# Second layer of a fused attention and mixture-of-experts kernel: 15 of 18 token tiles in Strassen's seven products, gated values through DRAM

## The chip, the cores and the metric

The kernel runs on one core of a Trainium2 chip. The metric is the device time of one execution in microseconds. Engines are named as in the profile: TensorE (PE; PEld for its weight loads), VectorE (DVE), ScalarE (ACT), GpSimd (POOL), and SyncE (SP), which only issues DMAs.

## The reference, cut to what matters

Attention (4 batches, 8 heads, 576 positions, 64 per head, causal, with a bias from a cumulative sum) gives x of 2304 tokens by 512. A mixture of 8 experts follows, two experts a token (512 to 1024 to 512). Its output goes into a second, dense layer, which is where the change lies:

```python
def _moe2_ref(x, w_gate, w_val, w_out):      # x [2304, 512], w_gate, w_val [512, 1536], w_out [1536, 512]
    gate = 1.0 / (1.0 + np.exp(-(x @ w_gate)))
    val = x @ w_val
    return (gate * val @ w_out).astype(np.float32)
```

## The kernel before, in words

Every matrix product is done in three passes of a reduced float32 format: an operand is split into a high part (a ScalarE copy) and a low part (a subtraction, on VectorE or GpSimd), and TensorE adds high x high, high x low and low x high in PSUM. So each product costs three matmuls and each operand one copy and one subtraction.

Four stages follow one another: attention with the gating of the experts (to about 279 us), the experts (`moe`, to 722 us), a branch for overfull experts that is normally not taken (`overflow`, L438 on), and the second layer (`moe2`, from 725.7 us to the end). Tokens go to their experts and back by indirect DMAs through DRAM; `ys` has two rows for each token, one per expert, to be added.

The experts run in units of one 128-wide block of one expert's hidden width: `mm1` (L214, matmuls at L225 to L227) for 640 slots, then `mm2` of the unit before (L239 to L241). The last expert is split: its first three slot tiles in one pass of eight units, its other two in the next eight, so that the second layer's first three token tiles can be read and transposed (`after`, L334) while the last units run. In the order of the code each unit also loads a later unit's weights (`load`: DMA on SP, high part on ScalarE at L151, low part mostly on GpSimd at L152), and runs a few steps of `background`, a generator that converts the second layer's weights, which arrive as 64-bit floats, in 24 halves of blocks (`convert`, L274): seven steps on VectorE to a float32, then the high part on ScalarE (L306) and the low part on VectorE (L309). Of the 12 blocks (128 of the hidden width each: 512 columns of w_gate, 512 of w_val, 512 of w_out) the first `RES` = 5 stay in SBUF (`wa`); 7 are stored to `w2d` in DRAM in split form and read back into `wc` by GpSimd's queue when the second layer begins (L577).

`moe2` works in 72 units: six groups of three token tiles (384 tokens), 12 blocks each. A unit n does `mm1` (2 x 4 x 3 matmuls of 384 columns into two PSUM banks, L539 to L541; sigmoid on ScalarE, the product and the split into `gh` and `gl` on VectorE and ScalarE) and then `mm2` of unit n-1 (3 tiles x 3 matmuls of 512 columns, L557 to L559), which adds into three PSUM banks over the 12 blocks. The next group's tiles are read (`fetch_sum`: a load on SP, then an adding load on GpSimd's queue) in units 1 to 3 and transposed by TensorE and split (`feed`) in units 7 to 9. All instructions of an engine run in the order in which the code issues them, and so do the DMAs of one queue; a buffer is taken again when its last user is done.

Of the kernel before, what the change touches and what calls it, by code (L numbers as in the profile page):

```python
# [19 lines left out]
FF2 = 1536  # L20
# [33 lines left out]
RES, AFTER = 5, 4  # L54
# [9 lines left out]
def attn_moe_moe2_kernel(ctx: ExitStack, tc: tile.TileContext, q, k, v, s, wgn, noise, wcat, w2cat, out):  # L64
# [66 lines left out]
    w2d = tc.dram_tile([FB2 - RES, 128, 2, FF2], F32, name="w2d")  # L131
# [7 lines left out]
    with res:  # L139
        w2, x0, first = moe(tc, moe_pools, res, gates, stage, ring, w1, late, count, xs, ys, wcat, w2cat, w2d, identf, identr)  # L140
        overflow(tc, xs, ys, wcat, carry, over, identf)
        moe2(tc, w2, x0, first, ys, w2d, identr, out)
# [13 lines left out]
def moe(tc, pools, res, gates, stage, ring, W, late, count, xs, ys, wcat, w2cat, w2d, identf, identr):  # L156

# [3 lines left out]
    wa = []  # L161
    with pools as ctx:
# [17 lines left out]
        def start(n):  # L180
            e, f = jobs[n][0:2]
            lo = nc.vector if n in LOW_DVE else nc.gpsimd
            pool, name = (w0, f"w{f}") if n < FB and f >= 4 else (ring, "w")
            LD[n] = weights(nc, tw[0] if n >= n_all - 2 else stage, pool, wcat, e, f, name, lo)
            next(LD[n])
# [88 lines left out]
        def convert(f, g, half=FF2 // 2):  # L274
# [8 lines left out]
            v = cv.tile([128, half], F32, name="cv")  # L283
# [15 lines left out]
            if f < RES:  # L299
                hi, lo = (wa[f][:, i, g * half:(g + 1) * half] for i in range(2))  # L300
            else:
                w = cv.tile([128, 2, half], F32R, name="cw", bufs=2)
                hi, lo = w[:, 0], w[:, 1]
            yield
            yield
            nc.scalar.activation(hi, v, AF.Copy)  # L306
            yield
            yield
# [3 lines left out]
            if f >= RES:  # L312
                stores.append(lambda: nc.sync.dma_start(w2d[f - RES][:, :, g * half:(g + 1) * half], f32(w)))
            yield
# [19 lines left out]
        def after(j):  # L334

            if j == 0:
                first.extend(x0.tile([128, 4, CT * 128], F32R, name=m) for m in ("xh", "xl"))
                for i in range(CT):
                    y[i] = fetch(nc, x0, ys, i, reads)
            for i in range(CT):  # L340
                if j == AFTER + i:
                    p = ps.tile([128, 512], F32, name=f"y{i}")
                    nc.vector.tensor_tensor(y[i][:, 0], y[i][:, 0], y[i][:, 1], op=OP.add)
                    turns[i] = feed(nc, y[i][:, 0], p, identf, *(x[:, :, i * 128:(i + 1) * 128] for x in first))
                if AFTER + i < j < AFTER + i + 3:
                    next(turns[i])

# [26 lines left out]
        for n in range(FB, n_all):  # L374
            e, f = jobs[n][0:2]
            if n == 2 * FB + 1:
                held.close()
                ra = res.enter_context(tc.tile_pool(name="res_a", bufs=1, side="right", reuse_waits="tile"))
                wa += [ra.tile([128, 2, FF2], F32R, name=f"wa{f2}") for f2 in range(RES)]
# [14 lines left out]
            if n == tail - 2:  # L394
                tw.append(ctx.enter_context(tc.tile_pool(name="tw", bufs=2, side="right", reuse_waits="tile")))
                for i in range(tail + 4, n_all):
                    start(i)
# [11 lines left out]
            if n == tail - 8:  # L409
# [3 lines left out]
                x0 = res.enter_context(tc.tile_pool(name="x0", bufs=1, side="right", reuse_waits="tile"))  # L413
        mm2s(n_all - 1)
        for j in range(FB, AFTER + CT + 3):
            after(j)
    rc = res.enter_context(tc.tile_pool(name="res_c", bufs=1, side="right", reuse_waits="tile"))
    for f2 in range(RES, FB2):
        wa.append(rc.tile([128, 2, FF2], F32R, name=f"wc{f2}"))
    return wa, x0, first  # L420
# [67 lines left out]
def fetch(nc, pool, ys, t, reads):  # L488

    y = pool.tile([128, 2, DM], F32, name="y", bufs=3)  # L490
# [612 lines left out]
```

## Time and profile before

| | |
|---|---|
| median of 3 runs | 1187.55 us (1185.42 to 1188.81) |
| the profiled execution: time, span | 1189.59 us, 1187.6 us |
| TensorE busy | 1136.2 us (96%) |
| VectorE, ScalarE, GpSimd busy | 592.5 us (50%), 433.8 us (37%), 291.1 us (25%) |
| mean granted TensorE clock | 0.984 |
| DMA | 162.59 MB, mean 137 GB/s |
| second layer | 725.7 us to the end |

Matmuls overlap, so a single one's duration (394 ns for 512 columns) is longer than the distance from one to the next, and TensorE's rate is read from the distances. A line's idle time is the time that its engine waited just before it. The granted clock is a share of 2.4 GHz: 1.00 is that level and 0.5 is 1.2 GHz.

### The profile page before, as it was taken

How to read it: one execution, taken by the hardware profiler on the slowest of the kernel's cores; microseconds unless marked ns; L12 is line 12 of the kernel's file. 1: busy time of each engine (PE TensorE's matmuls, PEld its weight loads, DVE VectorE, ACT ScalarE, POOL GpSimd, SP SyncE). 2: the span in 40 equal slices, each digit the busy share in tenths (PEclk: the TensorE clock that was granted, in tenths of full speed). 3: DMA queues.
4: the chain of work that ended last, by engine and by line, in shares of the span. 5: the costliest groups of instructions: out<-in, count | busy, mean ns of one | idle time of the engine just before them, and what ended most of it. 6: DMA issues, size and time to landing. Idle time of an engine off the chain costs nothing.

```text
span 1187.6 us, 17005 instructions
## 1 busy us (share of the span) xinstructions
PE 1136.2 (96%) x6625; PEld 998.2 (84%) x6625; DVE 592.5 (50%) x1030; ACT 433.8 (37%) x910; POOL 291.1 (25%) x286
## 2 busy tenths in 40 slices
PE   7998888799999999999999998999999999999998
PEld 4766655588999889888888997999999999999997
DVE  6787768473478988889882223121221221212111
ACT  6877666433334343333343432122121211212111
POOL 2103242423335353535353643000000000000000
PEclk8999989899999999999999999999999999999999
DMA  6898464426435546576744343803011030020000
GB/s 228 277 334 266 163 210 129 144 71 220 163 127 183 179 165 243 175 261 225 272 179 153 118 165 148 296 1 81 1 57 23 1 80 1 29 52 1 27 1 27
DMA packets 52606, 162.59 MB, mean 137 GB/s; under 512 B 6594, under 2 KB 7106, under 8 KB 51620
## 3 DMA queue, kind: packets, MB, share of 16 engines
q1 hardware_dynamic: 43060, 127.35, 32.3%
q0 software_dynamic: 9312, 33.90, 8.6%
q8 instruction: 54, 0.88, 0.3%
q14 instruction: 36, 0.29, 0.1%
q10 hardware_dynamic: 144, 0.16, 0.0%
HBM read 111.06 MB, written 46.44 MB: 133 GB/s over the span
## 4 chain that ended last, share of the span: by engine, by line
PE 68%; DVE 11%; DMA 7%; issue 5%; POOL 4%; ACT 3%; SPq 1%; another core or an unknown queue 0%; POOLq 0%; ACTq 0%; DVEq 0%
PE h L539 8%; PE h L541 8%; PE h L540 8%; PE o L558 4%; PE o L557 4%; PE o L559 4%; PE h L225 3%; PE h L227 3%; PE h L226 3%; PE y L239 3%; PE y L240 3%; PE y L241 3%; PE av L813 3%; PE tp L784 3%; DMA ys<-yo,row 3%
## 5 line engine op out<-in xcount | busy, mean ns | idle before, releaser
L152 POOL TENSOR_TENSOR w<-wraw,w 128x1024 fp32r<-128x1024 f32 x62 | 153.5, 2482 | 238.3 <-ACT w L151 233.3
L544 DVE TENSOR_TENSOR sg<-h,sg 128x384 f32<-128x384 f32 x72 | 40.2, 558 | 303.7 <-PE h L541 293.4
L225 PE MATMUL h<-xh,w 128*128 128x320 f32 (+2 forms) x512 | 162.1, 317 | 4.1 <-DVE hl L229 4.1
L227 PE MATMUL h<-xh,w 128*128 128x320 f32 (+2 forms) x512 | 158.6, 310 | 0.0
L226 PE MATMUL h<-xl,w 128*128 128x320 f32 (+2 forms) x512 | 158.3, 309 | 0.0
L239 PE MATMUL y<-w,hh 128*128 128x512 f32 x320 | 126.5, 395 | 0.0
L240 PE MATMUL y<-w,hh 128*128 128x512 f32 x320 | 126.3, 395 | 0.0
L241 PE MATMUL y<-w,hl 128*128 128x512 f32 x320 | 126.1, 394 | 0.0
L539 PE MATMUL h<-xh,wc 128*128 128x384 f32 x336 | 114.0, 339 | 0.0
L541 PE MATMUL h<-xh,wc 128*128 128x384 f32 x336 | 113.0, 336 | 0.0
L540 PE MATMUL h<-xl,wc 128*128 128x384 f32 x336 | 112.9, 336 | 0.0
L151 ACT ACTIVATE w<-wraw 128x1024 fp32r<-128x1024 f32 x68 | 72.0, 1059 | 104.1 <-PE y L241 79.9
L225 PEld LDWEIGHTS h<-xh,w 128*128 128x128 f32 x512 | 96.5, 188 | 8.1 <-DVE hl L229 6.4
L543 ACT ACTIVATE sg<-h 128x384 f32<-128x384 f32 x72 | 35.5, 493 | 184.8 <-PE h L541 184.8
L229 DVE SCALAR_TENSOR_TENSOR hl<-h,hh 128x320 fp32r<-128x320 f32 (+2 forms) x128 | 59.0, 485 | 86.4 <-ACT hh L228 86.4
L226 PEld LDWEIGHTS h<-xl,w 128*128 128x128 f32 x512 | 96.6, 189 | 1.6
L227 PEld LDWEIGHTS h<-xh,w 128*128 128x128 f32 x512 | 96.4, 188 | 0.0
L228 ACT ACTIVATE hh<-h 128x320 fp32r<-128x320 f32 (+2 forms) x128 | 54.9, 435 | 111.3 <-PE h L227 107.1
L546 ACT ACTIVATE gh<-sg 128x384 fp32r<-128x384 f32 x72 | 37.7, 524 | 155.9 <-DVE sg L544 155.9
L500 POOL DMA_DIRECT2D y<-ys x15 | 13.4, 995 | 294.7 <-PE h L541 284.9
L539 PE MATMUL h<-xh,wa 128*128 128x384 f32 x240 | 80.9, 337 | 3.3 <-ACTq L442 3.3
L541 PE MATMUL h<-xh,wa 128*128 128x384 f32 x240 | 80.8, 337 | 0.0
(202 smaller groups left out, 2420.0 us busy)
## 6 DMA issues: line engine op xcount, KB each, us to landing
wraw<-in_wcat_dram SPq DMA_DIRECT2D x68, 512.0 KB
dw<-in_w2cat_dram SPq DMA_DIRECT2D x24, 768.0 KB
w2d<-cw SPq DMA_DIRECT2D x14, 768.0 KB
wc<-w2d POOLq DMA_DIRECT2D x7, 1536.0 KB
xs<-zt SPq DMA_DIRECT2D x40, 258.0 KB
xr<-xs SPq DMA_DIRECT2D x40, 258.0 KB
qr<-in_q_dram SPq DMA_DIRECT2D x15, 640.0 KB
kr<-in_k_dram SPq DMA_DIRECT2D x15, 576.0 KB
```

Of the source, the lines that this page charges most:

```text
L151: nc.scalar.activation(w[:, 0], r, AF.Copy)
L152: (lo or nc.gpsimd).tensor_tensor(w[:, 1], r, f32(w[:, 0]), op=OP.subtract)
L225: nc.tensor.matmul(p, w[:, 0, k], xh[:, c, c0], start=c == 0, stop=False)
L226: nc.tensor.matmul(p, w[:, 0, k], xl[:, c, c0], start=False, stop=False)
L227: nc.tensor.matmul(p, w[:, 1, k], xh[:, c, c0], start=False, stop=c == 3)
L229: nc.vector.scalar_tensor_tensor(hl[:, c0], p, 0.0, f32(hh[:, c0]), op0=OP.max, op1=OP.subtract)
L239: nc.tensor.matmul(y, hh[:, k], w[:, 0, 512:], start=n % FB == 0, stop=False)
L240: nc.tensor.matmul(y, hh[:, k], w[:, 1, 512:], start=False, stop=False)
L241: nc.tensor.matmul(y, hl[:, k], w[:, 0, 512:], start=False, stop=n % FB == FB - 1)
L539: nc.tensor.matmul(q, w[:, 0, s], xh[:, c], start=c == 0, stop=False)
L540: nc.tensor.matmul(q, w[:, 0, s], xl[:, c], start=False, stop=False)
L541: nc.tensor.matmul(q, w[:, 1, s], xh[:, c], start=False, stop=c == 3)
```

## The change

The second layer's first three token tiles (the first group) are computed as before. The other 15 tiles get their first product in seven block products for eight: the sum over 512 is halved (gate rows g1, g2 and value rows v1, v2, each 256 by 128 for a block), and each token tile is halved into 64 and 64 tokens. The weights' operands are g1, g2, v2 and four sums s1 to s4; the tokens' operands are four halves and three differences. They are kept for two groups of tiles, of eight and of seven (`sizes`), so a product's matmuls have 512 or 448 columns.

A turn of the new loop does one block for one of the two groups, 24 turns in all. It issues the read of the next turn's weights (`combos`: 512 KB from `w2f` on SP; four GpSimd sums of 256 columns; high parts on ScalarE, 1792 columns in three pieces; low parts on VectorE), does six of its products on four PSUM banks, and the last product of the turn before (`pend`) as its third. Partial sums leave PSUM by three ScalarE copies (p1, p5, u2) and three VectorE additions; two sigmoids and two multiplications give the gated values, which SP stores to `gs` in DRAM. During the first eight-tile group's turns the second group's tiles are read, transposed and combined (`combine`). With turn 12 the first group's operands are given up and all of w_out is read into their place (`wo`). After the turns, `final` does each tile's output product alone (36 matmuls of 512 columns), with its gated values read from `gs` (`get`) and split (`parts`) two tiles ahead.

The converted weights are no longer split and kept in `moe`: every half block goes unsplit to `w2f`, and the first group reads and splits blocks as it goes (`block`), the first three in the last eight units of the experts. There the second layer's tiles are read by two loads each (`both`), and of the four last weights one more shares the raw buffers.

```diff
-            if f < RES:
-                hi, lo = (wa[f][:, i, g * half:(g + 1) * half] for i in range(2))
...
-            nc.scalar.activation(hi, v, AF.Copy)
...
-            nc.vector.tensor_tensor(lo, v, f32(hi), op=OP.subtract)
...
+            stores.append(lambda: nc.sync.dma_start(w2f[f][:, g * half:(g + 1) * half], v))
...
-                for i in range(tail + 4, n_all):
-                    start(i)
+                for i in (4, 5, 7):
+                    start(tail + i)
+            if n == tail + 2:
+                start(tail + 6)
...
+    def combos(self, u):
+        nc, r = self.nc, self.stage.tile([128, 1024], F32, name="wraw")
+        nc.sync.dma_start(r, self.w2f[u % FB2][:, 0:1024])
+        yield
+        g1, g2, v1, v2 = (r[:, i * 256:(i + 1) * 256] for i in range(4))
+        s = self.raw()
+        s1, s2, s3, s4 = (s[:, i * 256:(i + 1) * 256] for i in range(4))
+        for o, x, y, op in ((s1, v1, v2, OP.add), (s2, s1, g1, OP.subtract), (s3, g1, v1, OP.subtract),
+                            (s4, g2, s2, OP.subtract)):
+            nc.gpsimd.tensor_tensor(o, x, y, op=op)
+        yield
+        self.W["u", u] = w = self.slot(COMBO)
+        parts = (slice(0, 512), r[:, 0:512]), (slice(512, 768), v2), (slice(768, COMBO), s[:, 0:1024])
+        for c, x in parts:
+            nc.scalar.activation(w[:, 0, c], x, AF.Copy)
+        yield
+        for c, x in parts:
+            self.low(w, c, x)
+            yield
...
+        def combine(t):
+            p = ps.tile([128, 512], F32, name="tr", bufs=1)
+            turn(nc, Y.pop(t), p, identr)
+            k = two.yk.tile([128, 8, 2, 64], F32, name="xk")
+            nc.scalar.activation(k[:, 1:3].rearrange("p g c w -> p (g c) w"), p[:, :, 0], AF.Copy)
+            nc.scalar.activation(k[:, 0:4:3], p[:, :, 1].rearrange("p (g c) w -> p g c w", g=2), AF.Copy)
+            yield
+            for o, x, y in ((4, 0, 1), (5, 3, 4), (6, 3, 0), (7, 2, 5)):
+                nc.vector.tensor_tensor(k[:, o], k[:, x], k[:, y], op=OP.subtract)
+            yield
+            nc.scalar.activation(hi, k, AF.Copy)
+            yield
+            nc.vector.tensor_tensor(lo, k, f32(hi), op=OP.subtract)
...
+        for u in range(n_u):
+            if u + 1 < n_u:
+                two.start(two.combos, u + 1, key)
...
+            product(a, 0, 0, True)
+            p1 = copy(a, "p1", 2)
+            if s == 0 and 0 <= f - 2 < sizes[1]:
+                side = combine(sizes[0] + f - 2)
+                next(side)
+            two.go(key)
+            next(side, None)
+            product(c_, 3, 3, True)
+            p5 = copy(c_, "p5")
+            next(side, None)
+            pend()
+            if s == 0 and f < sizes[1]:
+                Y[sizes[0] + f] = two.fetch(CT + sizes[0] + f)
+            if u == FB2:
+                xc[0].close()
+                wo += [pool.tile([128, 2, 1024], F32R, name=f"wo{j}") for j in range(FB2 // 2)]
+                for j in range(FB2 // 2):
+                    nc.sync.dma_start(f32(wo[j][:, 1].rearrange("p (f n) -> p f n", f=2)),
+                                      w2f[2 * j:2 * j + 2, :, 1024:].rearrange("f p n -> p f n"))
+            if s == 1 and 0 <= f - 3 < FB2 // 2:
+                two.split(wo[f - 3], slice(0, 1024), f32(wo[f - 3][:, 1]))
+            two.go(key)
+            next(side, None)
+            product(b, 1, 1, True)
+            g1 = add(b, p1)
+            two.go(key)
+            product(a, 4, 4, False)
+            u2 = copy(a, "u2")
+            nc.scalar.activation(g1, g1, AF.Sigmoid)
+            two.go(key)
+            product(c_, 6, 2, False)
+            g2 = add(c_, u2)
+            nc.scalar.activation(g2, g2, AF.Sigmoid)
+            two.go(key)
+            product(a, 5, 5, False)
+            v2 = add(a, p5)
+            nc.vector.tensor_tensor(o[:, :, 1], g2.rearrange("p (t w) -> p t w", w=64),
+                                    v2.rearrange("p (t w) -> p t w", w=64), op=OP.mult)
+            if u >= n_u - 2:
+                get(u - n_u + 2)
+            def pend(f=f, s=s, a=a, g1=g1, o=o, product=product):
+                product(a, 2, 6, False)
+                nc.vector.tensor_tensor(o[:, :, 0], a.rearrange("p (t w) -> p t w", w=64),
+                                        g1.rearrange("p (t w) -> p t w", w=64), op=OP.mult)
+                nc.sync.dma_start(gs[f][:, s * 1024:s * 1024 + sizes[s] * 128], o.rearrange("p t h w -> p (t h w)"))
```

## Rows read from the trace of the kernel before

**Rows 1.** The page's chain that ended last: share of the span by engine.
```profile
PE 68%; DVE 11%; DMA 7%; issue 5%; POOL 4%; ACT 3%; SPq 1%; another core or an unknown queue 0%; POOLq 0%; ACTq 0%; DVEq 0%
```
**Rows 2.** Stretches: us, each engine's busy time (instructions), granted clock, DMA share, GB/s.
```profile
290.00:668.00 378.00, 372.25 (x2136) 333.60 (x2136) 284.48 (x394) 143.91 (x233) 158.28 (x109) 1.00 0.55 190
731.00:745.00 14.00, 13.73 (x72) 12.45 (x72) 3.26 (x6) 4.22 (x7) 5.60 (x9) 1.00 0.90 358
...
1075.00:1150.00 75.00, 75.00 (x402) 70.33 (x401) 16.07 (x28) 15.09 (x29) 0.00 (x0) 1.00 0.03 11
```
**Rows 3.** Timeline of TensorE, second layer: start, duration, line, form.
```profile
743.12 0.33 PE L539 MATMUL h<-xh,wa 128*128 128x384 f32 x1
...
749.36 0.33 PE L539 MATMUL h<-xh,wa 128*128 128x384 f32 x1
...
800.41 0.34 PE L539 MATMUL h<-xh,wa 128*128 128x384 f32 x1
...
804.65 0.39 PE L557 MATMUL o<-wc,gh 128*128 128x512 f32 x1
...
806.72 0.34 PE L539 MATMUL h<-xh,wa 128*128 128x384 f32 x1
```
**Rows 4.** Instructions by line: count, busy us, mean ns of one, idle before, releaser.
```profile
L152 POOL TENSOR_TENSOR w<-wraw,w 128x1024 fp32r<-128x1024 f32 x62 | 153.5, 2482 | 238.3 <-ACT w L151 233.3 <-DMA wraw<-in_wcat_dram 5.0
...
L151 ACT ACTIVATE w<-wraw 128x1024 fp32r<-128x1024 f32 x68 | 72.0, 1059 | 104.1 <-PE y L241 79.9 <-DMA wraw<-in_wcat_dram 18.4 <-issue 3.3
...
L309 DVE TENSOR_TENSOR cw<-cv,cw 128x768 fp32r<-128x768 f32 x14 | 23.2, 1654 | 2.5 <-ACT cw L306 2.1
...
L512 DVE TENSOR_TENSOR xl<-tr,xh 128x512 fp32r<-128x512 f32 x15 | 10.4, 692 | 18.3 <-ACT xh L510 18.3
...
L152 DVE TENSOR_TENSOR w<-wraw,w 128x1024 fp32r<-128x1024 f32 x6 | 7.3, 1222 | 2.0 <-ACT w L151 2.0
...
L573 ACT ACTIVATE oo<-o 128x512 f32<-128x512 f32 x11 | 6.5, 591 | 3.5 <-PE o L559 3.5
```
**Rows 5.** TensorE's waits, 290 to 668 us: us in total, times, longest.
```profile
PE h L225 <- DVE hl L229: 4.1, 7, 0.8
```
**Rows 6.** Pieces of the chain that ended last: start, us, what (DMAs: issue to landing).
```profile
458.68 5.20 DMA wraw<-in_wcat_dram
...
502.28 9.70 DMA dw<-in_w2cat_dram
...
673.92 3.56 DMA wraw<-in_wcat_dram
```
**Rows 7.** Timeline of ScalarE and of TensorE around the second layer's beginning.
```profile
708.54 1.06 ACT L151 ACTIVATE w<-wraw 128x1024 fp32r<-128x1024 f32 x1 [1.05 <-PE y L241]
...
725.69 0.44 PE L539 MATMUL h<-xh,wa 128*128 128x384 f32 x1 [3.25 <-ACTq L442]
```
**Rows 8.** Timeline of GpSimd and of VectorE in the experts' stage.
```profile
454.67 2.41 POOL L152 TENSOR_TENSOR w<-wraw,w 128x1024 fp32r<-128x1024 f32 x1 [6.57 <-ACT w L151]
...
496.45 4.78 POOL L152 TENSOR_TENSOR w<-wraw,w 128x1024 fp32r<-128x1024 f32 x2
...
455.10 0.69 DVE L207 TENSOR_TENSOR xl<-tr,xh 128x512 fp32r<-128x512 f32 x1 [2.34 <-ACT xh L206]
455.71 2.18 DVE L309 TENSOR_TENSOR cw<-cv,cw 128x768 fp32r<-128x768 f32 x1
...
496.21 5.45 DVE L289 TENSOR_SCALAR ca<-ca 128x768 int32<-128x768 int32 x1
```
**Rows 9.** Timeline of SP's queue in the experts' stage.
```profile
499.32 2.28 SPq L197 DMA_DIRECT2D xr<-xs  x5
```
**Rows 10.** DMA traffic from 498.9 to 512 us.
```profile
DMA packets 1419, 3.94 MB, mean 301 GB/s; under 512 B 142, under 2 KB 142, under 8 KB 1418
```
**Rows 11.** Two stretches around an idle time of TensorE in the attention stage.
```profile
229.20:231.35 2.15, 0.00 (x0) 0.00 (x0) 0.00 (x0) 1.21 (x4) 0.00 (x0) 0.50 0.27 44
231.35:236.00 4.65, 4.65 (x18) 3.23 (x20) 0.36 (x2) 2.20 (x6) 0.00 (x0) 0.51 0.92 304
```

More of the change, by code (lines that the diff above doesn't have):

```diff
@@ L412, in moe @@
                 conv.close()
-                x0 = res.enter_context(tc.tile_pool(name="x0", bufs=1, side="right", reuse_waits="tile"))
+                two = Second(tc, res, stage, ys, w2f)
         mm2s(n_all - 1)
-        for j in range(FB, AFTER + CT + 3):
+        for j in range(FB, FEED[-1] + 3):
             after(j)
[L417 to L420, printed above, removed]
+    return two, first
 def owners(nc, pool, e, x, n):
@@ new lines, in moe2 @@
+        n = 0
+        for f in range(FB2):
+            low = iter(())
+            if 0 <= f - LEAD < sizes[0]:
+                low = combine(f - LEAD)
+                for _ in range(3):
+                    next(low)
+            if f == FB2 - 1:
+                two.go("u0", 2)
+            mm1(f, low)
+            if f == FB2 - 1:
+                two.go("u0", 3)
+                break
+            if f:
+                mm2(f - 1)
+            while n < min(f + 3 - LEAD, sizes[0]):
+                Y[n] = two.fetch(CT + n)
+                n += 1
+            if 2 < f + 2 < FB2:
+                two.go(f + 2, 3)
+            if 2 < f + 3 < FB2:
+                two.start(two.block, f + 3, f + 3)
+            if f == FB2 - 3:
+                two.start(two.combos, 0, "u0")
+            if f == FB2 - 2:
+                two.go("u0")
@@ new lines, in moe2, with final @@
+        mm2(FB2 - 2)
+        one.close()
+        two.early.close()
+        tmp = ctx.enter_context(tc.tile_pool(name="m2t", bufs=1, side="right", reuse_waits="tile"))
+        ps = ctx.enter_context(tc.tile_pool(name="m2b", bufs=1, space=PSUM, reuse_waits="tile"))
+        wo = []
+        def final(t):
+            g = two.run.pop(("g", t))
+            o = ops.tile([128, DM], F32, name=f"o{t % 3}")
+            for f in range(FB2):
+                w = wo[f // 2][:, :, (f % 2) * DM:(f % 2 + 1) * DM]
+                last(o, [g[:, i] for i in range(2)], [w[:, i] for i in range(2)], slice(f * 128, (f + 1) * 128), f == 0,
+                     f == FB2 - 1)
+                yield
+            put(CT + t, o)
@@ new lines, in get, with parts @@
+        def get(t):
+            two.run["r", t] = r = two.raw()
+            nc.sync.dma_start(r.rearrange("p (f w) -> p f w", w=128), gs[:, :, t * 128:(t + 1) * 128].rearrange("f p w -> p f w"))
+        def parts(t):
+            r = two.run.pop(("r", t))
+            two.run["g", t] = g = two.slot(FF2)
+            for c in range(3):
+                c = slice(c * 512, c * 512 + 512)
+                two.split(g, c, r[:, c])
+                yield
+        n_u = 2 * FB2
+        pend = lambda: mm2(FB2 - 1)
```

260 lines of the change are left out of this document (170 added, 90 removed).

## The prediction

> **What bounds the kernel now.** I read the page's shares first: TensorE holds 68% of the chain that ended last, and nothing else more than 11% [rows 1]. A mean over stages can hide a stage with another limit, so the table of stretches came next [rows 2]. The reader is to see two things in it. In the second layer (from 725.7 us) TensorE is busy for the whole of a stretch, at the full granted clock (1.00, the 2.4 GHz level), while VectorE and ScalarE are busy for a fifth of it and GpSimd hardly. And in the experts' stretch before it TensorE leaves 5.75 of 378 us idle. So in the stage that changes, only fewer or shorter matmuls can save time, and there is room on the other engines. Third, the timeline of TensorE [rows 3]: one unit (one of 12 blocks of the hidden width for three token tiles) takes 6.31 us from 800.41 to 806.72: 24 matmuls of 384 columns in 4.24 us, 0.1767 each, then 9 of 512 in 2.07, 0.230 each. The unit at 743.12 takes 6.24. There are 72 such units, about as many of the one length as of the other.
>
> **Matmuls removed.** Fifteen of the 18 tiles, 60 units, give up the 24 matmuls of the first product: 60 x 24 = 1440 at 0.1767 = 254.4 us. In their place come 24 turns (12 blocks for 8 tiles, 12 for 7), each of seven products of 2 x 3 = 6 matmuls: 12 x 42 = 504 of 512 columns and 504 of 448. The former at 0.230 take 115.9 us; the latter at 0.2033, halfway between the two sizes that the rows show, 102.5. That is 218.4, or 36.0 less. From the 6.24 unit ((6.24 - 2.07)/24 = 0.174) it is 250.3 against 217.6, 33 less. I take **-34.5**. Seven products for eight would by columns alone give an eighth, 31 us; the rest is that fewer, longer matmuls pay the fixed part of each less often. The output product (540 matmuls of 512) and the transposes, four a tile, are the same as before and cancel.
>
> **Weights converted earlier.** Each half block's conversion loses a copy on ScalarE and a subtraction on VectorE, 24 times (the latter 1654 ns on average [rows 4]). In that stage TensorE waited 4.1 us in all for VectorE's hl [rows 5]: the gain is between 0 and 4.1, I take **-1.5**. The same splits come back in the last eight units of the experts and in the first token group.
>
> **Last units of the experts, and the boundary.** The seventh of the last weights now shares a raw buffer with the fifth, so its load can start only when GpSimd is done with that one: about 706.5, landing 3.6 to 5.2 later [rows 6], so at 710.1 to 711.7, while ScalarE took that load at 708.54 [rows 7]. ScalarE holds its Relu for 2 to 3 us and splits a third of a block beside it; the Relu has some 2.8 us until its matmuls come. 0 to 2, I take **+0.7**. The wait of 3.25 us before the second layer [rows 7] hangs on the branch that every engine takes and stays.
>
> **First group (three tiles, as before).** Per unit ScalarE now also splits a block (three parts of 512, 0.6 each by 591 ns for a copy of 512 and 1059 for one of 1024 [rows 4]) and makes a tile's combinations (two copies of 256, one of 896: 1.8 us): 1.8 + 1.8 + 1.0 = 4.6 of 6.3 us. VectorE, with 692 ns for 512 and 1222 for 1024 [rows 4], so 1.04 ns a column and 0.16 fixed: 3 x 0.69 + 4 x 0.29 + 1.1 + 2 x 0.56 = 5.4. Both fit and run a unit ahead. 0 to 4 for in-order mishaps; **+1**.
>
> **The turns, if nothing collides.** Take the second token group, products of 6 x 0.2033 = 1.22 us. TensorE's order is 1st, 2nd, the last product of the turn before, then 4th to 7th, ending at 8.54. VectorE adds g2 after the 6th (7.5 to 8.2), makes the low half of 1024 weights (1222 ns [rows 4]) until 9.4, adds v2 (0.69) and multiplies v2 by g2 (0.69) until 10.8, or 2.2 into the next turn. That multiplication frees the single buffer into which ScalarE copies p5 of the next turn, wanted at 2.6: in time. ScalarE: p5 copy until 3.2, next weights' high halves 0.6 + 0.4 + 1.06 until 5.3, u2 copy (591 ns) 6.3 to 6.9; the 7th product wants it at 7.32. Nothing stalls, with 0.4 us to spare.
>
> **What collides.** GpSimd makes four sums of 256 columns a turn, about 0.6 each at a quarter of 2.4 us (a sum of 1024) [rows 4], 2.5 in all. Where VectorE has both inputs in SBUF and GpSimd is at work, VectorE waits: the subtraction of 768 columns at 455.71, some 0.96 us of work, took 2.18 and ended 0.8 after GpSimd's sum (454.67, 2.41); an operation of 768 at 496.21 took 5.45, across two sums (496.45, 4.78). The one at 455.10, with an input in PSUM, took its usual 0.69 [rows 8]. The Trainium skill says the same and speaks against this change: by "SBUF — State Buffer", section "Who interferes with whom", a VectorE instruction with two SBUF inputs and a reading GpSimd instruction share a port pair, and "the second one to issue fully blocks". By that rule every turn can be hit, and the sum is that of the third rival below; with the port free whenever VectorE asks, this term would be nothing. When do the sums run? SP reads the weights of turn u+2 only after it has issued the store of turn u-1's gated values, about 5.1 into turn u. Landing takes 3.6 to 5.2 [rows 6]: 0.2 to 1.8 into turn u+1, and the sums last until 2.8 to 4.4. There stands the multiplication of v2 (1.5 to 2.2): it then ends at 3.5 to 5.1, the p5 copy at 4.1 to 5.7, the splits at 6.2 to 7.8, the u2 copy at 6.9 to 8.4, and the 7th product is 0 to 1.1 late. In six turns of this group 1.06 for the output weights' split comes before the splits, and it is 0.6 to 2.2 late. The first token group's turns are 1.1 longer, but seven of them carry a tile's combinations (1.8 on ScalarE): 0 to 1. If hit throughout: 6 x 1.4 + 6 x 0.5 + 12 x 0.4 = 17. If VectorE gets in between two sums (each second one depends on the one before): about 0. I take **+6**, nearer the lower end, as a single sum's delay of 0.6 is absorbed.
>
> **The output weights' load.** In turn 12, once the first token group's operands are free (3.7 into the turn), SP issues six loads of 512 KB into their place, and turn 14's weights are read behind them in the same queue. A queue serves in order: the 768 KB at 502.28, behind five reads of 258 KB [rows 9] and the store of line 313, landed after 9.70 us [rows 6]. Ahead of turn 14's weights are 0.46 + 3.1 MB, with their own 0.5 that is 4.1 MB, from about 4.8 on; at 358 GB/s [rows 2] 11.5 us, at the mean of 301 around the row of 9.70 [rows 10] 13.6: landing at 16.3 to 18.4. Then 2.5 for sums, 1.06 for the last split, 0.6 for the u2 copy: 20.5 to 22.6, where turn 13's 7th product wanted it at 8.54 + 7.32 = 15.9. Stall 4.6 to 6.7; take 6, as neither rate has the first byte's delay in full. An idle of such length lets the clock fall: in the idle before 231.35 it went to 0.50 (the 1.2 GHz level) and stayed there for 4.65 us of work [rows 11], so 2.3 us lost; take 2. Together **+8**; nothing if the loads find the data early, 11 at most.
>
> **Last stage.** Each tile's gated values come back as 768 KB in runs of 512 bytes. The third tile's read is issued behind the last store, some 7 to 9 us into the first tile's 8.3 us of matmuls, and is wanted 17 us into them. No row shows runs of 512 bytes. Between 3.6 (a load of 512 KB) and 9.7 (the row behind a queue), plus 1.4 for the first split, the stall is 0 to 3; later reads have two tiles' time. **+1**. Beside it: the Trainium skill ("DMA: Bandwidth & Descriptors", Specifications) puts the least size for full rate at 512 bytes, by which this would be nothing; no run here shows it yet.
>
> **Sum.** -34.5 - 1.5 + 0.7 + 1 + 6 + 8 + 1 = -19.3. The profiled execution took 1189.6 us (span 1187.6, 2.0 around it), so 1170.3; it is 2.0 above the median of the runs, 1187.55, and against that I forecast **1168 us**.
>
> **Rivals.**
> 1. *All hidden.* The burst's data come in time and no turn is hit: -34.5 - 1.5 = -36, 1152 us. For it: VectorE and ScalarE have a third of each turn free. Against: the order of SP's queue, in which I find no way around the burst.
> 2. *Slower: the read behind the store.* Place: SP's queue in each turn. The 7th product bears a landing of 7.32 - 0.1 - 0.6 - 1.06 - 2.5 = 3.1 into the turn, issued 3.4 before it: 6.5 us; in the first token group 8.3. If landings take the 9.70 of [rows 6], stalls are 12 x 3.2 + 12 x 1.4 = 55 us; with 9.2 of other costs, 1187.5 - 34.5 + 9.2 + 55 = 1217 us. It decides from a landing of 8.45 us on (12 x 1.95 + 12 x 0.15 = 25, all that is left of the gain). Against it: a turn moves 1 to 1.5 MB, 120 to 155 GB/s, where the experts' stage ran 190 [rows 2] with landings of 3.6 to 5.2.
> 3. *Hit throughout.* VectorE is shut out for the whole of GpSimd's four sums in every turn: 17 in place of 6, 1179 us. For it the row of 5.45 us [rows 8].
>
> **Numbers.** My forecast has 0.50 (1160 to 1177 its own range), the first rival 0.25, the third 0.13 (a quarter of it within 0.3% of before), the second 0.07; 0.05 is left for several terms at their upper ends, which comes out about even. A measurement of this kernel tells some 0.3%, 3.6 us, from no change. Faster: 0.50 + 0.25 + 0.10 = 0.85; same 0.08; slower 0.07. The range of 8 in 10 reaches from 1154, near the first rival, to 1184, past the third.
>
> **What would show it.** Matmuls of the turns 0.23 and 0.20 apart show the first term. A single idle of 5 to 8 us on TensorE in the second turn after the token groups change, ended by ScalarE's u2 copy, with the granted clock at 0.5 after it, shows the burst; smaller idles of about 0.5 ended by the same copy show collisions, and VectorE instructions with two SBUF inputs are then well over 1.04 ns per element. I am wrong if TensorE stalls in the first group or at the first turn, if the turns are spaced by anything other than TensorE, or if the last stage's reads are late at every tile.

## The result, and the profile after

The changed kernel took 1171.78 us (median of 4 runs, 1167.87 to 1177.41), the kernel before 1187.68 (4 runs): ratio 0.9872, 95% interval 0.9829 to 0.9915, so it is faster, by about 1.3%. Forecast were 1168 us, 1154 to 1184. The profiled execution took 1167.87 us, its span is 1166.1, against 1187.6 before.

The page's chain of waits, which answers to [rows 1], and three stretches, which answer to [rows 2] (us, busy time of PE, PEld, DVE, ACT and POOL with counts, granted clock, DMA share, GB/s):

```profile
PE 36%; DMA 1%; ACT 1%; DVE 0%; issue 0%; POOL 0%; ACTq 0%; POOLq 0%; SPq 0%
```
```profile
290.00:668.00 378.00, 378.00 (x2165) 341.57 (x2165) 249.39 (x369) 129.32 (x208) 167.95 (x117) 1.00 0.57 192
...
983.35:991.85 8.50, 8.50 (x44) 7.88 (x43) 6.15 (x10) 5.40 (x9) 3.32 (x5) 1.00 0.35 116
1050.00:1150.00 100.00, 100.00 (x430) 80.60 (x429) 26.33 (x42) 22.98 (x42) 0.00 (x0) 1.00 0.44 119
```

DVE fell from 11% of the chain to nothing. TensorE now has no idle at all in the experts' stretch, where it had 5.75 us, and none in a turn (second line) or in the last stage (third). The timeline of TensorE, to be read against [rows 3]: the first matmul of a turn of the first token group and of the next turn, then the same for the second group.

```profile
894.10 0.39 PE L759 MATMUL c<-xc,w 128*128 128x512 f32 x1
...
903.90 0.39 PE L759 MATMUL c<-xc,w 128*128 128x512 f32 x1
...
991.85 0.36 PE L759 MATMUL c<-xc,w 128*128 128x448 f32 x1
...
1000.34 0.36 PE L759 MATMUL c<-xc,w 128*128 128x448 f32 x1
```

A turn of 42 matmuls takes 9.80 us, 0.2333 a matmul, and then 8.49, 0.2022 a matmul. What TensorE still waits for after the 690th us, where it is more than 0.25 us (idle and releaser in brackets):

```profile
697.80 0.50 PE L244 MATMUL y<-w,hh 128*128 128x512 f32 x1 [0.94 <-ACT hh L233]
...
700.35 0.79 PE L246 MATMUL y<-w,hl 128*128 128x512 f32 x1 [1.81 <-DVE hl L234]
...
703.43 0.90 PE L576 MATMUL y<-identf,y 128*128 128x128 f32 x3 [1.01 <-DVE y L343]
...
717.83 0.66 PE L643 MATMUL h<-xh,w 128*128 128x384 f32 x1 [4.08 <-PEq L446]
...
808.69 0.61 PE L759 MATMUL a<-xc,w 128*128 128x512 f32 x1 [3.02 <-ACT u L765]
...
945.15 0.74 PE L759 MATMUL a<-xc,w 128*128 128x448 f32 x1 [6.93 <-ACT u L765]
...
1036.76 0.47 PE L759 MATMUL a<-xc,w 128*128 128x448 f32 x1 [1.41 <-DVE p L769]
```

That is the whole list: the end of the experts, the boundary, the first turn, turn 13 (turns are counted from 0), the last turn. The two executions compared stretch by stretch, each from the start of a matmul to the start of another (the experts have 79 runs of first-layer matmuls, which serve as marks and are counted from 0):

| stretch | before | after | difference | forecast |
|---|---|---|---|---|
| attention, to the experts' first matmul | 244.85 | 237.66 | -7.2 | 0 |
| to the 20th run | 96.90 | 96.37 | -0.5 | 0 |
| 20th to 60th run | 297.79 | 289.57 | -8.2 | -1.5 |
| 60th to 76th run | 71.57 | 71.68 | +0.1 | 0 |
| 76th run to the second layer | 14.58 | 22.55 | +8.0 | +0.7 |
| second layer | 461.9 | 448.3 | -13.6 | -18.5 |

The sum is -21.4. In attention no line differs, and its length turned out to depend on the occasion (first experiment); without it the change is worth -14.3 us in the profile, where -19.3 was forecast. So a third of what this one profile shows can't be put down to the change.

### The profile page after: what moved, and what is told of

Read it like the earlier page. It is cut to its first block, busy times and chain, and to the rows that moved or that the text cites. A ratio compares the mean times of both kernels' runs of the same rounds, so it can differ in the third digit from the quotient of the medians.

```text
span 1166.1 us, 16824 instructions
## 1 busy us (share of the span) xinstructions
PE 1108.5 (95%) x6193; PEld 940.4 (81%) x6193; DVE 714.8 (61%) x1227; ACT 527.3 (45%) x1073; POOL 368.9 (32%) x375
## 5 line engine op out<-in xcount | busy, mean ns | idle before, releaser
L521 DVE TENSOR_TENSOR w<-ro,w 128x512 fp32r<-128x512 f32 (+1 forms) x105 | 88.0, 875 | 55.8 <-ACT w L517 55.6
L759 PE MATMUL a<-xc,w 128*128 128x512 f32 (+1 forms) x192 | 74.3, 387 | 11.4 <-ACT u L765 9.9
L1022 ACT ACTIVATE pt<-sc,nm 128x128 f32<-128x128 f32 (+3 forms) x128 | 66.4, 527 | 31.0 <-DVE nm L1005 25.0
L761 PE MATMUL a<-xc,w 128*128 128x512 f32 (+1 forms) x192 | 74.3, 387 | 0.0
L760 PE MATMUL a<-xc,w 128*128 128x512 f32 (+1 forms) x192 | 74.2, 386 | 0.0
L246 PEld LDWEIGHTS y<-w,hl 128*128 128x128 f32 x320 | 60.5, 189 | 16.8 <-DVE hl L234 2.7
L546 POOL TENSOR_TENSOR ro<-wraw 128x256 f32<-128x256 f32 x48 | 41.6, 867 | 100.6 <-DMA wraw<-w2f 68.0
L675 PE MATMUL o<-wo,w 128*128 128x512 f32 x180 | 71.2, 396 | 0.0
L676 PE MATMUL o<-wo,w 128*128 128x512 f32 x180 | 71.2, 395 | 0.0
```

Of the source, the lines that this page charges most:

```text
L246: nc.tensor.matmul(y, hl[:, k], w[:, 0, 512:], start=False, stop=n % FB == FB - 1)
L675: nc.tensor.matmul(o, gh[:, c], wl, start=False, stop=False)
L676: nc.tensor.matmul(o, gl[:, c], wh, start=False, stop=stop)
L759: nc.tensor.matmul(b, w[:, 0, k], xh[:, j, c], start=start and c == 0, stop=False, skip_group_check=True)
L760: nc.tensor.matmul(b, w[:, 0, k], xl[:, j, c], start=False, stop=False, skip_group_check=True)
L761: nc.tensor.matmul(b, w[:, 1, k], xh[:, j, c], start=False, stop=c == 1, skip_group_check=True)
```

## The experiments

Each variant starts from the changed kernel. Turns and the middle of the experts' stage repeat to some 0.02 us from run to run where an edit does not touch them, so a stretch or a turn tells more than the whole time does. The ratios are to the kernel before on the same occasion.

**Attention: the kernel before once more.** No edit.

> The kernel before, unchanged, for a second profile of its attention stage, in which no line differs between the two kernels: TensorE's first matmul of the experts began at 244.85 us before and at 235.1 to 237.7 us in the five profiles of the changed kernel and its variants. Theory: that is scatter from execution to execution, and this profile has it between 235 and 241 us. Rival: the change itself moves it (other places of tiles and of the DRAM tensors); then it is 243 to 246 us again.

1193.35 us; the experts began at 248.40, later than either theory said. But the other three kernels of that occasion, all changed ones, began them at 247.72, 245.48 and 246.60, and the four of a later occasion on the same chip at 228.53 to 235.89. So the stage varies by up to 20 us from occasion to occasion and by 1 to 7 within one, whichever kernel runs; the -7.2 can't be put down to the change. Whether some tenths or even 3 us of it are the change's stays open: on the one occasion with both, the kernel before was the latest of the four, by 0.7 to 2.9 us.

**Eight products for seven.**

```diff
             product(c_, 6, 2, False)
+            product(c_, 6, 2, False)
```

> The changed kernel, but each turn makes the product of u2's sum twice, so eight products a turn instead of seven (the output is then not the reference's). Theory: TensorE alone paces the turns, at 0.2333 us for a matmul of 512 columns and 0.2022 for one of 448: the turns of the first token group get 1.40 us longer (9.80 becomes 11.2), those of the second 1.21 (8.49 becomes 9.70), 24 turns 31.4 us; the two idles, of 3.02 us in the first turn and of 6.93 in turn 13, shrink by what the other engines then have more time, 1.4 and 2.4, so about 27 to 29 in all. Rival: the turns are paced by the engines beside it or by the weights' landing; then they get longer by less than 0.5 us each, 12 us in all.

The turns took 11.20 and 9.71 us, +1.40 and +1.21 as TensorE's pace says (1206.78 us, ratio 1.0115, 1.0077 to 1.0154). The stage of turns got 26.7 us longer; the two idles shrank to 1.63 and 5.44. Apart from these two, TensorE alone paces the turns.

**One output tile for the first three results.**

```diff
...
-            e = two.oo.tile([128, DM], F32, name="oo")
+            if e is None:
+                e = two.oo.tile([128, DM], F32, name="oo")
...
+                k = two.yk.tile([128, 8, 2, 64], F32, name="xk").rearrange("p g c w -> p (g c w)")
                 for t in range(CT):
-                    put(t, O[t])
+                    put(t, O[t], k[:, (t - 1) * DM:t * DM] if t else None)
```

> The changed kernel, but with the first three tiles' results evicted into three tiles of their own (two halves of a tile that is free then) instead of one tile after another. Theory: in the changed kernel one output tile makes the three evictions wait for each other's DMA, the third blocks ScalarE's queue, and so the first turn's 7th product waits 3.02 us and then runs at a lower clock (about 1.65 us more): both go, 1171.8 becomes about 1167, and the first turn lasts 9.8 us like the others. Rival: ScalarE is late in that turn by the work it has there (two blocks of splits and combinations); then the idle stays between 2 and 3 us and the time within 1 us of the changed kernel.

ScalarE's timeline in the first turn, of the changed kernel and then of this one:

```profile
800.13 0.60 ACT L668 ACTIVATE oo<-o 128x512 f32<-128x512 f32 x1
805.78 0.60 ACT L668 ACTIVATE oo<-o 128x512 f32<-128x512 f32 x1 [5.05 <-PE c L761]
...
808.05 0.59 ACT L765 ACTIVATE u<-a 128x512 f32<-128x512 f32 x1
```
```profile
798.77 0.60 ACT L669 ACTIVATE oo<-o 128x512 f32<-128x512 f32 x1
800.14 0.60 ACT L669 ACTIVATE xk<-o 128x512 f32<-128x512 f32 x1 [0.77 <-PE o L677]
...
...
802.94 0.60 ACT L767 ACTIVATE u<-a 128x512 f32<-128x512 f32 x1 [0.43 <-PE a L763]
```

The row puts the 5.05 us down to TensorE, which was long done; what came late was the tile, in use by two evictions and their DMAs one after the other. With three tiles the idle is gone and the first turn lasts 11.86 us (a turn and the last nine matmuls of the first group) in place of 16.70: 4.84 us, of which 3.02 were the wait and the rest matmuls at a lower clock after it. (1162.45 us, ratio 0.9836, 0.9801 to 0.9871.)

**The output weights' loads, one a turn.**

```diff
-                for j in range(FB2 // 2):
-                    nc.sync.dma_start(f32(wo[j][:, 1]...), w2f[2 * j:2 * j + 2, :, 1024:]...)
+            if s == 1 and f < FB2 // 2:
+                nc.sync.dma_start(f32(wo[f][:, 1]...), w2f[2 * f:2 * f + 2, :, 1024:]...)
```

> The changed kernel, but with the six 512 KB loads of the output weights issued one in each of turns 12 to 17 instead of all six in turn 12. Theory: turn 14's weights wait in SP's queue behind the six, and that alone costs the idle of 6.93 us in turn 13 and some 1.8 of lower clock after it: 8.7 us less, about 1163. Rival one: the wait is moved on and split up, as each turn's weights still stand behind 512 KB (landing 1.5 to 3 us later than now, against a slack of some 3 us in this group): six idles of 0 to 1.5 us, 1163 to 1170. Rival two: the idle is not the loads' but the change of token group's (a new set of operands, tiles closed and opened): it stays, 1171.

1159.87 us, ratio 0.9812 (0.9781 to 0.9843). Turn 13 went from 17.39 to 8.48 us, and the first rival holds in part: the wait is smaller, and some of it moves on. Turns 15, 17 and 18 took 10.22, 9.08 and 9.09, so 6.0 of the 8.9 us come back. What was spread, SP's queue and ScalarE in the changed kernel:

```profile
927.21 3.81 SPq L794 DMA_DIRECT2D wo<-w2f  x6
931.13 0.46 SPq L539 DMA_DIRECT2D wraw<-w2f  x1
...
940.04 0.94 ACT L551 ACTIVATE w<-wraw 128x512 fp32r<-128x512 f32 x2 [6.09 <-DMA wraw<-w2f]
943.61 1.06 ACT L551 ACTIVATE w<-ro 128x1024 fp32r<-128x1024 f32 x1 [2.63 <-POOL ro L546]
944.57 0.53 ACT L765 ACTIVATE u<-a 128x448 f32<-128x448 f32 x1
```

The seventh load is issued 3.9 us after the sixth other one began, ScalarE has its data 8.9 us later, and the u2 copy stands behind both splits in ScalarE's queue.

**The seventh weight's own buffer.**

```diff
-            LD[n] = weights(nc, tw[0] if n == n_all - 1 else stage, ...)
+            LD[n] = weights(nc, tw[0] if n >= n_all - 2 else stage, ...)
-                for i in (4, 5, 7):
+                for i in (4, 5, 6, 7):
...
-            if n == tail + 2:
-                start(tail + 6)
...
```

> The changed kernel, but with the seventh of the last weights in a raw buffer of its own and its load issued early, as before the change (the room for it comes from moving a tile of the second layer to another pool). Theory: ScalarE's wait of 4.28 us for that load, the two subtractions of GpSimd that then stand back to back and VectorE's four operations of 2.5 us beside them cost the 6.9 us that the last units of the experts lose against the kernel before: most of it comes back, 5 to 7 us, about 1165 to 1167; and the idle before the second layer may be shorter. Rival: the loss is the splits of the second layer's weights, now done in these units on ScalarE and VectorE: then 0 to 2 us come back.

**The last four low parts on VectorE.**

```diff
-LOW_DVE = (3, 5, 6, 7, 16, 17)
+LOW_DVE = (3, 5, 6, 7, 16, 17, 76, 77, 78, 79)
```

> The changed kernel, but the low parts of the last four weights of the experts are made by VectorE (1.22 us each) instead of GpSimd (2.4 us each). Theory: in the last units VectorE's operations of 512 columns with two inputs in SBUF take 2.5 instead of 0.69 us because GpSimd's subtraction holds them off for its whole length; without GpSimd they take 0.69, the shared raw buffer comes free 1.2 us earlier, TensorE's idles of 0.94, 1.81 and 1.01 us get shorter and 3 to 5 us of the 6.9 lost come back, about 1167. Rival: the order behind the seventh weight's late load alone costs the time: 1 to 1.5 us come back, and the operations on VectorE stay at about 2.5 us or its queue is late for TensorE instead.

From the 76th run to the 78th the kernel before takes 6.43 us, the changed one 13.21, with the own buffer 8.69, with the low parts moved 10.78, with both (last experiment) 7.49. So of the 6.8 lost the own buffer gives 4.5 back, the low parts 2.4, and both together 5.7: the two causes overlap, and 1.1 stay lost. In the first run the rival of 0 to 2 falls, though less came back than the 5 to 7 expected. In the second neither number came: ScalarE still waits 4.54 us for the load, but the subtractions take 0.69 us as the theory said. (1162.24 us, 0.9841, 0.9806 to 0.9877; 1176.13 us, 0.9875, 0.9843 to 0.9906.) GpSimd, ScalarE and VectorE there in the changed kernel, then VectorE with the low parts moved:

```profile
697.04 5.18 POOL L158 TENSOR_TENSOR w<-wraw,w 128x1024 fp32r<-128x1024 f32 x2 [3.73 <-ACT w L157]
...
695.90 1.06 ACT L157 ACTIVATE w<-wraw 128x1024 fp32r<-128x1024 f32 x1 [4.28 <-DMA wraw<-in_wcat_dram]
...
697.51 2.44 DVE L521 TENSOR_TENSOR w<-ro,w 128x512 fp32r<-128x512 f32 x1 [3.32 <-ACT w L517]
699.88 0.41 DVE L234 SCALAR_TENSOR_TENSOR hl<-h,hh 128x256 fp32r<-128x256 f32 x1
700.21 2.56 DVE L521 TENSOR_TENSOR w<-ro,w 128x512 fp32r<-128x512 f32 x1
```
```profile
705.46 1.23 DVE L158 TENSOR_TENSOR w<-wraw,w 128x1024 fp32r<-128x1024 f32 x1 [4.22 <-ACT w L157]
706.60 0.69 DVE L521 TENSOR_TENSOR w<-ro,w 128x512 fp32r<-128x512 f32 x1
707.20 0.42 DVE L234 SCALAR_TENSOR_TENSOR hl<-h,hh 128x256 fp32r<-128x256 f32 x1
```

VectorE's subtraction of 512 columns takes 2.5 us while GpSimd subtracts and 0.69 while it does not, and hl waits behind it. The Trainium skill ("SBUF — State Buffer", section "Who interferes with whom") says that a VectorE instruction with two SBUF inputs and a reading GpSimd instruction exclude one another, and that the one that issues second is blocked for as long as the first lasts; this trace agrees, with 2.44 and 2.56 us on VectorE behind GpSimd's two in 5.18.

**The split put back into the experts' stage**, whole, then the copy alone, then the subtraction alone.

```diff
             nc.vector.tensor_tensor(v, v, f32(u), op=OP.add)
+            yield
+            yield
+            hi = cv.tile([128, half], F32R, name="chi")
+            nc.scalar.activation(hi, v, AF.Copy)                              # not in e10
+            yield
+            yield
+            nc.vector.tensor_tensor(f32(a), v, f32(hi), op=OP.subtract)       # e10: f32(u) for f32(hi); not in e9
...
-            for _ in range(4):
-                yield
+            yield
```

The number of steps (`yield`) stays the same; the half block's store is issued three steps later in all three variants, so the subtraction's 0.15 us hold that delay too.

> The changed kernel, but with a copy on ScalarE and a subtraction on VectorE of 768 columns put back into each of the 24 conversions in the experts' stage, into scratch that nobody reads; stores and loads are unchanged. Theory: the 8.75 us that the stretch of the experts from about 240 to 690 us gained come from these operations' absence (VectorE busy 284 us there instead of 249): it gets 6 to 9 us longer, with TensorE's idles for VectorE's hl and ScalarE's copies of tokens back, about 1179. Rival: the gain is that only one value per weight goes to DRAM instead of two (less DMA traffic, and the tokens' reads come sooner): then the stretch gets 0 to 2 us longer. My forecast had 0 to 4.1.

> The changed kernel, with only the copy of 768 columns on ScalarE put back into each of the 24 conversions. Put back together with the subtraction on VectorE, it made the stretch between the 20th and the 60th group of first-layer matmuls 9.69 us longer (299.26 in place of 289.57; the kernel before: 297.79). Theory: VectorE's queue is what fills up, as it is 82 to 85% busy there with the subtraction and 74% without: the copy alone costs 0 to 1.5 us. Rival: ScalarE's copy holds up hh, and hl behind it: 4 us or more.

> The changed kernel, with only the subtraction of 768 columns on VectorE put back into each of the 24 conversions (it reads other scratch, so that it waits for no other engine). Theory: it stands ahead of hl in VectorE's queue and costs most of the 9.69 us by itself, 6 to 10. Rival: what costs is that VectorE waits for ScalarE's copy in the middle of the conversion (2.1 to 4.4 us of idle are put down to it): then the subtraction alone costs 3 to 6 us.

The stretch from the 20th to the 60th run took 299.26 us with both, 292.34 with the copy, 289.72 with the subtraction, 289.57 with neither. (1177.68 us, ratio 0.9963, 0.9943 to 0.9983, with both; 1167.84 and 1158.84 for the others, one run each.) The gain is the split's and not the smaller DMA traffic's: with the split put back and the traffic left small, the stretch is even 1.5 us longer than before the change. But why it costs what it does is told by none of the numbers expected of the parts: the copy alone costs 2.77 us, between theory and rival, and the subtraction alone 0.15, below both. VectorE's load by itself, my theory, falls. TensorE's row of 350 to 630 us, with both and with the subtraction alone, and then ScalarE's wait for the copy's input and TensorE's wait for hl in that stretch (us in total, times, longest), each with both and with the copy alone:

```profile
350.00:630.00 280.00, 272.87 (x1551) 244.15 (x1550) 237.31 (x309) 106.27 (x172) 127.11 (x88) 1.00 0.59 201
```
```profile
350.00:630.00 280.00, 280.00 (x1605) 252.73 (x1604) 234.84 (x301) 96.04 (x155) 126.24 (x89) 1.00 0.61 201
```
```profile
ACT chi L307 <- DVE cv L303: 65.8, 21, 5.9
PE h L230 <- DVE hl L234: 4.5, 8, 1.1
```
```profile
ACT chi L307 <- DVE cv L303: 51.9, 17, 4.9
PE h L230 <- DVE hl L234: 0.4, 1, 0.4
```

VectorE is about as busy in the first as in the second (237 and 235 us), and TensorE loses 7.1 us in one and nothing in the other. So the copy has to be there. It waits in ScalarE's queue for VectorE's result, some 3 us each time, and what stands behind it is late. In the kernel before the wait is the same:

```profile
ACT cw L306 <- DVE cv L298: 39.6, 13, 5.6
ACT wa L306 <- DVE cv L298: 21.1, 7, 5.0
```

These 60.7 us of ScalarE stood in the trace, as the idle time of an engine 39% busy. But the copy's wait alone is not the cause either: it is nearly as long with the copy alone, and there TensorE waits only 0.4 us for hl. With both, only two of the eight waits for hl (0.87 and 1.09 us) go from the copy by a late hh to a late hl, as in the first two lines here. In the other six (2.6 us together) hh had been done for 2.7 us or more, and hl stood behind the conversion's steps in VectorE's queue, as in the last three, where one step took 3.05 us instead of 0.96; in two of the six VectorE had waited 2.40 us before that for tokens' copies (xh), which stand behind the conversion's copy on ScalarE.

```profile
563.52 0.85 ACT L307 ACTIVATE chi<-cv 128x768 fp32r<-128x768 f32 x1 [5.39 <-DVE cv L303]
564.72 0.89 DVE L234 SCALAR_TENSOR_TENSOR hl<-h,hh 128x320 fp32r<-128x320 f32 x2 [1.29 <-ACT hh L233]
...
509.25 0.44 ACT L233 ACTIVATE hh<-h 128x320 fp32r<-128x320 f32 x1 [1.26 <-PE h L232]
506.87 3.05 DVE L296 SCALAR_TENSOR_TENSOR cu<-dw,ca 128x768 int32<-128x768 int32 x1
512.89 0.88 DVE L234 SCALAR_TENSOR_TENSOR hl<-h,hh 128x320 fp32r<-128x320 f32 x2
```

So copy and subtraction cost far more together (9.69) than apart, with the two engines waiting for one another (VectorE for the copy 4.4 us in nine waits). Which step of this makes up the difference stays open.

**GpSimd's sums twice and three times.**

```diff
-            nc.gpsimd.tensor_tensor(o, x, y, op=op)
+            for _ in range(3):                       # 2 in e11
+                nc.gpsimd.tensor_tensor(o, x, y, op=op)
```

> The changed kernel, with each of GpSimd's four sums of 256 columns a turn made twice, some 3.2 us more a turn. From the trace of the changed kernel: in the second token group the sums end 0.8 us before ScalarE takes the split that reads them, that chain has 0.4 us to the u2 copy, and the copy ends 1.6 before the 7th product wants it: a margin of 2.8 to 2.9; in the first token group 4.7. Theory: the turns bear nearly all of it, 0 to 0.4 us per turn of the second group, 0 to 4 us in all, and the idle of turn 13 grows by up to 3.2. Rival (VectorE is held off by GpSimd's sums whenever both read SBUF, and there is more of it now): VectorE's operations of two SBUF inputs take 1.5 us and more, and the turns of both groups get longer by 0.5 us or more, 12 us or more in all.

> The changed kernel, with each of the four sums made three times, some 6.4 us more a turn. Theory: this passes the margin of 2.8 to 2.9 us in the second token group by 3.5 and that of 4.7 in the first by 1.7. A turn that ends late gives the next one's sums, which began before its end, as much more time, so the mean is half of the excess: 1.75 x 11 + 0.85 x 10 = 28 us, with turns that alternate or settle. Rival one: no such return, 3.5 x 11 + 1.7 x 10 = 55 us. Rival two: the sums are hidden and the turns stay at 9.8 and 8.5 us, 0 to 4 us.

1197.74 and 1250.73 us (ratios 1.0149, 1.0080 to 1.0217, and 1.0598, 1.0536 to 1.0660); the stage of turns got 27.6 and 86.8 us longer, so no number expected held but the 12 us or more of the first run's rival, and mostly not by its reason. The turns of the first group with tiles to combine took 10.5 to 11.4 us instead of 10.2 with the sums twice. The turns 14 to 22 took 8.49 to 12.97 us with the sums twice, short and long ones alternating, 10.3 on average and 12.5 with three. GpSimd and ScalarE in one long turn of the former, cut to the start and the end of the chain:

```profile
1010.04 0.84 POOL L546 TENSOR_TENSOR ro<-wraw 128x256 f32<-128x256 f32 x1 [3.07 <-DMA wraw<-w2f]
...
1013.02 0.73 POOL L547 TENSOR_TENSOR ro<-ro,wraw 128x256 f32<-128x256 f32 x1
...
1014.54 1.61 POOL L547 TENSOR_TENSOR ro<-wraw 128x256 f32<-128x256 f32 x1
1016.10 1.19 POOL L546 TENSOR_TENSOR ro<-wraw,ro 128x256 f32<-128x256 f32 x1
...
1018.20 1.06 ACT L552 ACTIVATE w<-ro 128x1024 fp32r<-128x1024 f32 x1 [3.39 <-POOL ro L547]
1019.16 0.53 ACT L766 ACTIVATE u<-a 128x448 f32<-128x448 f32 x1
```

The chain is the one that the forecast drew: landing, sums, split, u2 copy, 7th product. But the sums are not 3.2 us longer; they last 8.1 instead of 3.4, 4.7 more, and that is past the margin of 2.9 by 1.8. The turns of the second group lost as much on average (10.3 against 8.49), the turn shown 2.7 and its short neighbours 0.7 to 0.8. A sum takes 0.73 us alone and 1.2 to 1.6 beside VectorE's operations with both inputs in SBUF (the subtractions of the splits, a multiplication). Of these the subtractions of 512 columns of a turn's weights take 0.80 on average there, those of 256 0.67 and those of 1024 1.25, against 0.68, 0.44 and 1.22 in the changed kernel. So a collision does exist in the turns, and with the sums twice GpSimd bears more of it. With three, GpSimd works 11 to 12 us in a turn and the chain paces it.

**All mended.** The edits above together, the output weights' split moved to the end of a turn, and

```diff
-        for _ in range(3):
-            next(fin)
-            next(p)
+        for i in range(7):
+            next(fin)
+            if i < 3:
+                next(p)
```

> All that the first runs point to, together: the first three tiles' results in tiles of their own, the output weights' loads one a turn with their split moved to the end of a turn, the seventh weight's own buffer and early load, the last four low parts on VectorE, and seven instead of three steps of the first output tile ahead of the last product. Theory: the parts add up, as they are far from each other: against the changed kernel 4.8 us in the first turn, 8.9 in turn 13, 5 to 6.5 in the last units, 1.4 in the last turn, 20 to 21.6 us in the profile, so about 1150. Rival: the split at a turn's end delays VectorE's multiplication in the next turn, or the wait comes back elsewhere: six idles of 0.3 to 1.5 us, 1152 to 1158.

1157.42 us against 1193.01 of the kernel before on the same occasion: ratio 0.9707, interval 0.9671 to 0.9744, wholly below the changed kernel's. It beats both. The time is 7 us above the 1150 expected and within the rival's 1152 to 1158, but not by the rival's reason: in its profile the experts began at 246.60, 8.9 us later than in the changed kernel's, and the six idles are not there. From the 16th run of the experts on, which leaves attention out, it takes 841.5 us, the changed kernel 861.1 and the kernel before 874.9: 19.6 less than the changed one, where 20 to 21.6 were expected. After the boundary one idle is left on TensorE in the whole second layer:

```profile
PE a L760 <- ACT u L766: 0.3, 1, 0.3
```

Three turns (13, 15 and 17) are still 0.3 to 0.6 us too long; no run shows why.

## Why the prediction was right, and where only its sum was

The time fell in the range and near the forecast, and the mechanism of the main term was right. That the sum came so near is in part luck: experts, boundary, first turn and collisions were mis-sized by -6.7, +7.3, +4.8 and -6 us, which nearly offset one another, and attention happened to be 7.2 us shorter in the profile after. By the prediction's steps:

- **Matmuls removed, -34.5: right.** By the distances after, 504 x 0.2333 + 504 x 0.2022 = 219.5 us against 218 forecast; with 0.1755 for a matmul before (the mean of its 0.1767 and 0.174; 252.7) it is -33.2. The eight-product run shows that nothing else paces the turns that don't stall. The output product did not quite cancel: its 540 matmuls are 0.2333 apart in stretches of their own and were 0.230 in [rows 3], 1.8 us, for which no cause was found.
- **Weights converted earlier, -1.5: mis-sized; -8.2.** I bounded it by the 4.1 us that TensorE's waits for hl add up to [rows 5]. Two things were missing: the two idles for tokens' reads (1.6 us), and the part of a stall that the view doesn't put down as idle: 5.75 us of idle in 350 to 630 stood for 8.2 of length, presumably since a matmul's modelled end of 0.31 to 0.39 us covers some of it. The experiments show that the time is the split's, and that neither its copy nor its subtraction costs it alone. The row of 5.45 us [rows 8], from which I drew the collisions of the turns, belongs here: TensorE's wait of 0.83 us at 504.69 is for the hl that stands behind it in VectorE's queue, with hh done at 500.37.
- **Last units and boundary, +0.7: mis-sized; +8.0.** The load came at 695.90 by a wait of 4.28 us as the mechanism said, and I let ScalarE's slack of 2.8 us absorb it. I left out what happens behind it: the splits, now done in these units, meet two GpSimd subtractions back to back, and VectorE is held off here as I had expected it in the turns. That is 6.8 of the 8.0. The wait at the branch did not stay at 3.25 either; it was 4.08, and 3.7 to 4.2 in all variants.
- **First group, +1: nothing was lost there** but 2.0 us of lower clock behind the branch, and the first turn cost 4.84 us that no term had. The prediction worked out engines' loads and missed that the output tiles went from three buffers to one. "Wrong if TensorE stalls at the first turn" stands in it, and it did.
- **Collisions, +6: they happen and cost nothing.** No turn stalls but the first, turn 13 and the last; the turns have a margin of 2.9 us. GpSimd's sums take 0.87 us on average instead of 0.73, which is 0.6 a turn, and the multiplication named in the prediction is held off in the first group's turns, though hardly in the second's (0.70 us). Here it is over the first group, with both inputs in SBUF, and then the other multiplication, which has one in PSUM:

```profile
L820 DVE TENSOR_TENSOR gv<-u,p 128x512 f32<-128x512 f32 x12 | 12.3, 1028 | 1.1
...
L827 DVE TENSOR_TENSOR gv<-a,p 128x512 f32<-128x512 f32 x12 | 8.3, 690 | 9.6 <-PE a L761 9.3
```

So the prediction had the right place, and not what it costs: 0.3 us on average, absorbed, as it says itself of a single sum's delay. Two slips stand in its working: the terms written for "hit throughout" add up to 16.2 and not 17, and the operation of 5.45 us [rows 8] is a TENSOR_SCALAR with one tensor input, so it is no example of two inputs in SBUF.

- **Output weights' load, +8: right; 8.90.** One idle of 6.93 us in turn 13, ended by the u2 copy, then 4.23 us for 12 matmuls of 0.2022 at a granted clock of 0.56, 1.8 lost to it. Six loads issued one a turn take it away.
- **Last stage, +1: no stall** between tiles, 8.40 us each; the last turn's 1.41 us were not foreseen.

For the second layer these come to -33.2 + 1.8 + 2.0 + 4.8 + 8.9 + 1.4 = -14.3, where -13.6 was measured.

Of the rivals, "hit throughout" and "the read behind the store" are out: a weights' read in the second group, issued at 987.05, lands within 4.2 us, half of the 8.45 from which it would have decided:

```profile
987.05 0.37 SPq L539 DMA_DIRECT2D wraw<-w2f  x1
...
991.29 0.73 POOL L546 TENSOR_TENSOR ro<-wraw 128x256 f32<-128x256 f32 x1 [5.10 <-DMA wraw<-w2f]
```

"All hidden" was nearer for the turns than my forecast, apart from turn 13.

## What to carry to other kernels

A helper's split on engines that were 39 and 85% busy cost 9.7 us of TensorE's time when it was put back, though its copy alone cost 2.8 and its subtraction alone 0.2: read what an off-path engine waits for, not only its busy share, and try the parts of an edit together as well as apart. When buffers get fewer to make room, follow each into the queue of the engine that waits for it. And spread a burst of loads over the turns, or the next turn's own read stands behind it.

## What was not expected of the hardware

The same idle of 3.02 us in the first turn cost differently from run to run: the granted clock in the four microseconds around its end was 0.62 in the changed kernel, 0.50 with the own buffer and 1.00 with the split in the experts, and the turn took 16.70, 17.54 and 15.14 us. In the four microseconds after the branch it was 0.50 to 0.62 at idles of 3.7 to 4.2 us, and in the kernel before 1.00 at 3.25. An idle of 1.46 us (the spread loads' turn 15) left it at 1.00. So a wait of 3 to 4 us costs from nothing to 2.7 us more than itself, the changed kernel's second layer began 2.0 us slower by that, and a difference of that size between single profiles says nothing of an edit.
